# The tail of an attention and routed-MLP kernel: one-tensor statistics, column groups with a pick matmul, ranks by a ones matmul, register-addressed row stores, hinted branches

## The chip, the cores and the metric

One core of a Trainium2 chip. The metric is the time of one execution on the device in microseconds (us), as the median of several executions; beside it stand the range and, where it matters, the mean granted clock of TensorE (1.0 is full speed). Kernels are compared within a call, on one chip, each in turn with the kernel before. A ratio is the mean time of one kernel's fast executions over that of the kernel before in the same rounds, so it is not quite the ratio of the medians that are quoted. "Same" means that the 95% interval of the ratio lies within 2%.

## The reference

Layer norm, attention with 16 query heads on one key and value head, a residual; then a second layer norm and an MLP that runs for only 8 of the 2048 rows, those with the largest router value.

```python
S, D, H, F, C = 2048, 448, 16, 1792, 8          # bf16 throughout
def A(x, wq, wk, wv, wo):                       # attention, one K/V head
    q = heads(x @ wq); k = x @ wk; v = x @ wv
    p = softmax(q @ k.T * (D // H) ** -0.5)
    return merge(p @ v) @ wo
def B(x, w_r, w_gate, w_up, w_down):            # MLP on 8 rows
    r   = x @ w_r
    idx = argsort(-r)[:C]
    y   = (silu(x[idx] @ w_gate) * (x[idx] @ w_up)) @ w_down
    return x.at[idx].add(y * sigmoid(r[idx]))
h  = x + A(layernorm(x), ...)
h2 = h + B(layernorm(h), ...)
```
(Shortened: batch dimension and index arithmetic left out. The second statement uses the layer norm both as input and as residual of B.)

## The kernel before: the parts concerned

The kernel gives every instruction to a small planner (`G.op`: engine, function, estimated duration in ns, what it reads and writes), which orders each engine's program. 281 exponentials on ScalarE carry the attention; VectorE and GpSimd make a share of the exponentials by integer arithmetic. When the last query block is done, the 8 rows are chosen and the MLP runs. TensorE is given matmuls on zeros where the plan shows it idle.

```python
# statistics of one tile of 128 rows, 15 times (in the trace: L752)
G.op(DV, lambda e: e.scalar_tensor_tensor(st[:, t, 6:7], mv[:, t, 0:1], -1.0, st[:, t, 4:5],
                                          ALU.mult, ALU.mult), 80, ...)
# candidates of the first 15 tiles: cast of their router values, transpose, top 8 of each, two small DMAs
G.op(DV, lambda e: e.tensor_copy(rp[:, 0:NT1], r_col[:, 0:NT1]), 80, ...)
...
dma(crow[0:1, :].rearrange("o (t k) -> o t k", k=8), c8[:, :], ["crow"], reads=["c8"])
...
dma(cidx[:, :], i8f[:, :], ["cidx"], reads=["i8f"])
# after the last tile: rank of each candidate, one-hot matrices, selected rows
G.op(DV, stt(scr128[0:8, :], ps[0:8, rbank, 0:128], cols[:, 2:3], onesb[0:8, :], ALU.is_gt, wst[0:8, 9:10]), 280, ...)
# ... gate and up projections on four column groups, silu, product, transposes ...
for h in range(2):                      # down projection: 16 matmuls, 8 columns of the array each
    pieces([mm(ps[0:8, dbank, 0:D], guT[0:CK, k, 32 * c:32 * c + 8], wd_sb[0:CK, 4 * c + k, :],
               k == 0 and c == 0, k == 3 and c == 3) for k in (2 * h, 2 * h + 1) for c in range(4)], 8, 189, ...)
...
G.op(DV, lambda e: e.tensor_copy(base8, ps[0:8, 2, 0:D]), 531, ...)
G.op(DV, lambda e: e.scalar_tensor_tensor(rows8, ps[0:8, dbank, 0:D], fin[:, 1:2], base8, ALU.mult, ALU.add), 540, ...)
evs.append(G.op(PO, lambda e: e.indirect_dma_start(out=out[0], out_offset=...(ap=idx2[:, 0:1], axis=0),
                                                   in_=rows8, ...), 1000, ...))
# at the end of every engine: a flag decides whether an exact second program has to run
bad = e.value_load(flag[0:1, 0:1])
with e.If(bad != 0):
    ...
```
(Cuts are marked with dots.)

## Time and profile before

| | before |
|---|---|
| time, 3 executions | 393.47 us (393.27 to 393.99) |
| span of the profiled execution (it took 394.32 us, more than these three) | 392.5 us, mean granted clock 0.991 |
| first exponential starts, last one ends | 10.06, 370.77 us |
| tail, from there to the end of the span | 21.74 us |

What bounds the kernel is read in the prediction.

```profile
PEclk9999999999999999999999999999999999799999
```

The one slice below 9 is the 35th, where ScalarE has its only two gaps of over 0.3 us after the start.

### The profile page before, as it was taken

Reading aid. Unit: us, or ns where it says so; the run is one execution under the profiler, and the core shown is the slowest. Engines: PE = TensorE matmul, PEld = TensorE weight load, DVE = VectorE, ACT = ScalarE, POOL = GpSimd, SP = SyncE. Lnnn points to the kernel's source line nnn. Section 1 sums busy time; section 2 is a strip of 40 time slices with the busy share of each in tenths; the row PEclk is TensorE's granted clock in tenths of the full one; section 3 lists DMA queues with packets and bytes.
Section 4 is the critical chain, followed back from the end, with each engine's and each line's share of the span. In section 5 each row is a group of like instructions: output and inputs, shape, how many; then the busy total and the mean of one; then the engine's idle time right before and its main releaser. Section 6 shows DMA issues by size and latency. Waiting matters only on the chain.

```text
span 392.5 us, 8604 instructions
## 1 busy us (share of the span) xinstructions
PE 319.9 (82%) x3501; PEld 110.6 (28%) x3501; DVE 338.5 (86%) x695; ACT 366.7 (93%) x307; POOL 193.4 (49%) x180
## 2 busy tenths in 40 slices
PE   8899887878787888878787878888787878788794
PEld 4454322323232222223231322222232312122242
DVE  6995888989898998989898989989898989879872
ACT  5799999999999999999999999999999999799850
POOL 7410135646555464656365454646563654456410
PEclk9999999999999999999999999999999999799999
DMA  7993000010102010100102010100101020100110
GB/s 210 234 244 86 11 17 15 14 52 4 63 5 63 3 52 13 34 33 5 61 3 65 3 63 4 49 16 29 39 4 62 3 65 3 60 3 3 47 42 10
DMA packets 19892, 17.59 MB, mean 45 GB/s; under 512 B 6326, under 2 KB 17094, under 8 KB 19846
## 3 DMA queue, kind: packets, MB, share of 16 engines
q1 hardware_dynamic: 19781, 16.95, 15.8%
q8 instruction: 30, 0.49, 0.6%
q14 instruction: 17, 0.13, 0.1%
q0 software_dynamic: 64, 0.02, 0.0%
HBM read 11.44 MB, written 5.53 MB: 43 GB/s over the span
## 4 chain that ended last, share of the span: by engine, by line
DVE 60%; PE 23%; ACT 12%; issue 4%; POOL 0%; POOLq 0%
DVE Y L910 28%; PE ps L478 22%; ACT P L885 12%; DVE Y L919 11%; DVE st L752 2%; DVE Q L596 2%; DVE hbuf L730 2%; DVE Ot L932 2%; DVE junk L766 2%; DVE bn L734 2%; DVE bn L609 1%; DVE xnT L653 1%; DVE xx L638 1%; DVE mv L735 1%; DVE K L670 1%
## 5 line engine op out<-in xcount | busy, mean ns | idle before, releaser
L885 ACT ACTIVATE P<-ps 128x1536 bf16<-128x1536 f32 (+1 forms) x281 | 355.2, 1422 | 5.0 <-PE ps L478 4.5
L910 DVE TENSOR_SCALAR Y<-ps 128x512 int16<-128x512 f32 x240 | 164.0, 683 | 32.7 <-PE ps L478 32.6
L921 POOL TENSOR_TENSOR Y<-Y,step 128x1024 int32<-128x1024 int32 x60 | 113.5, 1892 | 142.7 <-DVE Y L919 142.1
L478 PE MATMUL ps<-Q,K 32*128 32x512 bf16 x1024 | 111.5, 385 | 62.6 <-DVE Y L910 45.8
L478 PE MATMUL ps<-Y,Vs 128*32 128x512 bf16 x960 | 89.6, 387 | 2.4 <-DVE Y L919 0.5
L478 PEld LDWEIGHTS ps<-Q,K 32*128 32x128 bf16 x1024 | 33.2, 91 | 177.8 <-ACT P L885 160.2
L919 DVE TENSOR_SCALAR Y<-Y 128x2048 int16<-128x2048 int16 x120 | 82.3, 696 | 0.6
L478 PE MATMUL ps<-P,Vs 128*32 128x512 bf16 x784 | 73.0, 388 | 0.0
L478 PE MATMUL ps<-zero 128*32 128x512 bf16 (+3 forms) x162 | 51.4, 395 | 1.2 <-DVE zero L497 1.2
L478 PEld LDWEIGHTS ps<-Y,Vs 128*32 128x32 bf16 x960 | 23.3, 94 | 33.3 <-issue 17.9
L713 POOL TENSOR_TENSOR On<-Ot,Rb 128x256 bf16<-128x256 f32 x28 | 19.8, 727 | 15.2 <-DMA Rb<-l_scr 15.2
L478 PEld LDWEIGHTS ps<-P,Vs 128*32 128x32 bf16 x784 | 18.8, 94 | 28.7 <-issue 26.7
L738 POOL TENSOR_TENSOR st<-st,nhalf 128x1 f32<-128x1 f32 x15 | 17.8, 1185 | 4.6 <-DVE st L736 4.6
L478 PEld LDWEIGHTS ps<-zero 128*32 128x32 bf16 (+1 forms) x162 | 14.4, 101 | 14.8 <-issue 7.5
L478 PE MATMUL ps<-xnT,wq_pad 112*128 112x128 bf16 x256 | 17.4, 220 | 0.0
L758 POOL TENSOR_SCALAR xx<-hbuf,st 128x448 bf16<-128x448 f32 x15 | 15.6, 1041 | 0.0
L478 PEld LDWEIGHTS ps<-xnT,wq_pad 112*128 112x128 bf16 x256 | 14.4, 98 | 3.6 <-issue 3.4
L478 PE MATMUL ps<-wo_pad,On 128*128 128x448 bf16 x64 | 15.0, 355 | 0.0
L755 POOL TENSOR_SCALAR xx<-hbuf,st 128x448 bf16<-128x448 f32 x15 | 11.2, 746 | 1.6
L730 DVE TENSOR_TENSOR hbuf<-ps,xx 128x448 f32<-128x448 f32 x15 | 9.4, 623 | 2.3 <-PE ps L478 2.3
L596 DVE TENSOR_SCALAR Q<-ps,qone 128x512 bf16<-128x512 f32 x15 | 11.2, 744 | 0.0
L752 DVE SCALAR_TENSOR_TENSOR st<-mv,st 128x1 f32<-128x1 f32 x15 | 11.1, 738 | 0.0
(179 smaller groups left out, 170.1 us busy)
## 6 DMA issues: line engine op xcount, KB each, us to landing
Rb<-l_scr SPq DMA_DIRECT2D x14, 256.0 KB
x_scr<-xx SPq DMA_DIRECT2D x15, 224.0 KB, 2.5
out_dram<-xx SPq DMA_DIRECT2D x16, 112.0 KB, 1.7
wg_sb<-in_B_w_gate_dram SPq DMA_DIRECT2D x1, 1568.0 KB, 14.3
wu_sb<-in_B_w_up_dram SPq DMA_DIRECT2D x1, 1568.0 KB, 20.5
wd_sb<-in_B_w_down_dram SPq DMA_DIRECT2D x1, 1568.0 KB, 25.4
xx<-in_A_x_dram SPq DMA_DIRECT2D x3, 448.0 KB, 5.5
wq_sb<-in_A_wq_dram SPq DMA_DIRECT2D x2, 196.0 KB, 2.9
```

The costliest lines, as they stand in the source:

```text
L478: return lambda e: e.matmul(o, lhsT=l, rhs=r, start=start, stop=stop)
L596: G.op(DV, lambda e: e.tensor_scalar(Q[:, q, :, :].rearrange("p g n -> p (g n)"), ps[:, bank, :], qone[:, 0:1], None, ALU.add), dvt(512), ...
L713: G.op(PO, lambda e, c=c: e.tensor_tensor(On[:, rb, c], Ot[:, rb, c], Rb[:, rb, c], ALU.mult), 750, reads=[both[h], rk[h]], writes=[("On", ...
L730: G.op(DV, lambda e: e.tensor_tensor(hbuf[:, hr, :], ps[:, bank, 0:D], x_sb[:, t, :], ALU.add), dvt(D), reads=[pk(bank), ("x", t)], writes ...
L738: G.op(PO, lambda e: e.tensor_tensor(st[:, t, 4:5], st[:, t, 7:8], nhalf[:, 0:1], ALU.pow), 600, reads=[("st7", t), "nhalf"], writes=[("st ...
L752: G.op(DV, lambda e: e.scalar_tensor_tensor(st[:, t, 6:7], mv[:, t, 0:1], -1.0, st[:, t, 4:5], ALU.mult, ALU.mult), 80, reads=[("mv", t), ...
L755: G.op(PO, lambda e: e.tensor_scalar(outf[:, t, :], hbuf[:, hr, :], st[:, t, 5:6], st[:, t, 6:7], ALU.mult, ALU.add), 800, reads=[("h", hr ...
L758: G.op(PO, lambda e: e.tensor_scalar(xn[:, t, :], hbuf[:, hr, :], st[:, t, 4:5], st[:, t, 6:7], ALU.mult, ALU.add), 800, reads=[("h", hr), ...
L885: G.op(AC, lambda e: e.activation(P[:, s0:s0 + w, :], ps[:, b0:b0 + w, :], ACT.Exp, bias=-(ZERO + SHIFT) * OCT, scale=OCT), w * 427 + 50, ...
L910: G.op(DV, lambda e: e.tensor_scalar(Y[:, y, 0, q, :].bitcast(I16), ps[:, vb, :], 0.0, 32639.0 - STEP[3], ALU.max, ALU.min), dvt(512), rea ...
L919: done = [G.op(DV, lambda e, c=c: e.tensor_single_scalar(y[c].bitcast(I16), y[0].bitcast(I16), STEP[c], ALU.add), 600, reads=r, writes=[(" ...
L921: G.op(PO, lambda e: e.tensor_tensor(y[3].bitcast(I32), y[0].bitcast(I32), step3[:, 0:1].broadcast_to([128, 1024]), ALU.add), 2050, reads= ...
```

## The change

Its intent: shorten the chain after the last exponential, and free the statistics of a form that stands behind GpSimd (up to 1.85 us a call in the profile before, 0.15 at its shortest). In words: a one-column statistic is computed by the form with a per-partition scalar instead of two tensors. Two small DMAs become masked products that matmuls sum. The rank of a candidate is counted by a matmul with ones. The down projection runs on four groups of 32 columns of the array, side by side, each leaving a partial sum; a small fp32 matmul with a "pick" matrix adds the four, scales each row by its sigmoid and adds it to its base row. Eight DMAs with the row number in a register store the rows. Each engine announces its last branch some operations ahead (a hint), to shorten the time from the branch to the next instruction (2.7 us on ScalarE in the profile before). The core of the diff:

```diff
-        G.op(DV, lambda e: e.scalar_tensor_tensor(st[:, t, 6:7], mv[:, t, 0:1], -1.0, st[:, t, 4:5],
-                                                  ALU.mult, ALU.mult), 80,
+        G.op(DV, lambda e: e.tensor_scalar(st[:, t, 6:7], mv[:, t, 0:1], st[:, t, 4:5], -1.0, ALU.mult, ALU.mult),
+             80,
...
-        G.op(DV, lambda e: e.tensor_copy(rp[:, 0:NT1], r_col[:, 0:NT1]), 80, ...)      # router values now go into rp directly
-        dma(crow[0:1, :].rearrange("o (t k) -> o t k", k=8), c8[:, :], ["crow"], reads=["c8"])
+        G.op(DV, lambda e: e.tensor_tensor(spread, bmask, c8[:, :].unsqueeze(1).broadcast_to([NT1, NT1, 8]), ALU.mult), ...)
+        G.op(PE, mm(ps[0:1, VB, 0:NC1], onesb[0:NT1, 0:1], wq_sb[0:NT1, 3, 0:NC1], True, True), 60, ...)
...
-    G.op(DV, stt(scr128[0:8, :], ps[0:8, rbank, 0:128], cols[:, 2:3], onesb[0:8, :], ALU.is_gt, wst[0:8, 9:10]), 280, ...)
+    G.op(PE, mm(ps[0:8, kbank, 0:1], above, onesb[:, 0:1], True, True), 64, ...)
...
-        pieces([mm(ps[0:8, dbank, 0:D], guT[0:CK, k, 32 * c:32 * c + 8], wd_sb[0:CK, 4 * c + k, :],
-                   k == 0 and c == 0, k == 3 and c == 3) for k in (2 * h, 2 * h + 1) for c in range(4)], 8, 189, ...)
+        for k in (2 * h, 2 * h + 1):
+            G.op(PE, [mm(ps[32 * c:32 * c + 32, dbank, 0:D], guT[0:CK, k, 32 * c:32 * c + 32], wd_sb[0:CK, 4 * c + k, :],
+                         k == 0, k == 3) for c in range(4)], 189, mode="V", ...)
...
+    G.op(PE, [mm(ps[:, rbank, 0:1], rep4(128, 0), rsig[:, 1:2], True, False),          # sigmoid of each row, on four groups
+              mm(ps[:, rbank, 0:1], rep4(8, 1), cols[:, 1:2], False, True),
+              mm(ps[0:1, rbank, 8:16], rsig[:, 0:1], ohf[:, 0, 0, 0:8], True, False),  # row numbers, on one partition
+              mm(ps[0:1, rbank, 8:16], cols[:, 0:1], ohf[0:8, 1, 0, 0:8], False, True)], 600, mode="F", ...)
+    G.op(DV, lambda e: e.tensor_scalar(pick8, mask8, ps[:, rbank, 0:1], None, ALU.mult), 90, ...)
...
+    for h, c in enumerate(halves):                                                     # fp32, into the bank of the base rows
+        G.op(PE, mm(ps[0:8, obank[h], 0:224], pick8, part[:, c], False, True), 390, mode="F", ...)
+        G.op(DV, lambda e, h=h, c=c: e.tensor_copy(rows8[:, c], ps[0:8, obank[h], 0:224]), 300, ...)
-    evs.append(G.op(PO, lambda e: e.indirect_dma_start(...), 1000, ...))
+    for j in range(8):                                                                 # four on SyncE, four on ScalarE
+        o = G.op(q, lambda e, j=j: e.dma_start(out[0, bass.ds(row[j], 1), :], rows8[j:j + 1, :]), 60, ...)
...
-                with e.If(bad != 0):
+                go = e.br_ne(bad, 0, on_true="exact_" + eng, on_false="end_" + eng)
+                go.branch_hint(hint)                     # announced {PE: 12, ScalarE: 8, VectorE: 8, GpSimd: 1, SyncE: 6} operations ahead
```
(Cuts are marked with dots; comments behind `#` in the diff are added here. Two further one-column statistics, not shown, change from the two-tensor form in the same way.)

## The prediction

> **What bounds the kernel now.** I read the page's head (busy shares and slices), then the costliest groups with their idle times, then the waits and the timeline of the two places where the bound lets go, last the lines of the closing branch.
>
> ```profile
> PE 319.9 (82%) x3501; PEld 110.6 (28%) x3501; DVE 338.5 (86%) x695; ACT 366.7 (93%) x307; POOL 193.4 (49%) x180
> ACT  5799999999999999999999999999999999799850
> L885 ACT ACTIVATE P<-ps 128x1536 bf16<-128x1536 f32 (+1 forms) x281 | 355.2, 1422 | 5.0 <-PE ps L478 4.5
> ```
>
> ScalarE is the bound until the last exponential ends at 370.8 us: 355.2 us of exponentials and only 5.0 us of idleness before them. Work saved on other engines is worth nothing there, except where ScalarE has to wait. The ACT row dips once inside the loop, in the 35th slice. The timeline shows why:
>
> ```profile
> 334.44 0.15 DVE L750 TENSOR_SCALAR st<-st 128x1 f32<-128x1 f32 x1
> 334.44 1.89 POOL L921 TENSOR_TENSOR Y<-Y,step 128x1024 int32<-128x1024 int32 x1
> 334.51 1.85 DVE L752 SCALAR_TENSOR_TENSOR st<-mv,st 128x1 f32<-128x1 f32 x1
> ...
> 337.10 0.40 PE L478 MATMUL ps<-Q,K 32*128 32x512 bf16 x4 [2.17 <-DVE Y L910]
> ...
> 337.54 4.04 ACT L885 ACTIVATE P<-ps 128x1536 bf16<-128x1536 f32 x3 [1.35 <-PE ps L478]
> ```
>
> A one-column VectorE operation lasts 1.85 us because it stands behind a GpSimd operation; PE waits 2.17 us for the bank that VectorE frees late, and ScalarE 1.35 us for PE. The table by stretch adds an after-effect: TensorE's granted clock is 1.00 before, 0.79 in 335 to 340 and 0.61 in 340 to 346, and ScalarE waits again at 342.08 (0.50) and 345.27 (0.23).
>
> After 370.8 nothing overlaps: the end is a chain of short steps, 21.7 us long, to the span's 392.5. Its last part:
>
> ```profile
> 384.32 3.19 PE L478 MATMUL ps<-wd_sb,Y 112*8 112x448 bf16 x16
> ...
> 387.55 0.67 DVE L1148 SCALAR_TENSOR_TENSOR Y<-ps,wq_sb,Y 8x448 bf16<-8x448 f32 x1 [2.92 <-PE ps L478]
> 389.22 0.92 POOL L1150 DMA_INDIRECT out_dram<-Y,wq_sb  x1 [11.52 <-DVE Y L1148]
> ```
>
> Sixteen down-projection matmuls, one each 0.189 us, use 8 of the array's 128 columns; then one pass, then a row store through GpSimd which lands 2.8 us after its issue (DMA part of the page). From the end of L1148 (388.22) to the end of the span it is 4.29 us.
>
> [...] of the two kinds side by side,
>
> ```profile
> L750 DVE TENSOR_SCALAR st<-st x15: 140/144/154, 75.7 to 368.2; 128x1 f32<-128x1 f32 x15
> ...
> L752 DVE SCALAR_TENSOR_TENSOR st<-mv,st x15: 147/751/1846, 75.8 to 368.3; 128x1 f32<-128x1 f32 x15
> ```
>
> the first never exceeds 154 ns, the second (two tensors in) has a median of 751.
> [...] Here
>
> ```profile
> L1216 ACTq COMPARE_BRANCH  x1: 45/45/45, 385.0 to 385.0; - x1
> L1216 PEldq COMPARE_BRANCH  x1: 3702/3702/3702, 385.0 to 385.0; - x1
> L1216 DVEq COMPARE_BRANCH  x1: 76/76/76, 388.1 to 388.1; - x1
> ...
> L1190 ACTq DRAIN  x1: 81/81/81, 387.7 to 387.7; - x1
> ...
> L1190 DVEq DRAIN  x1: 96/96/96, 391.3 to 391.3; - x1
> ```
>
> ScalarE reaches its next instruction 2.7 us after its branch, VectorE 3.2 us, PE stays 3.7 us in it. All of that hides today behind the store.
> [...] The trace shows the fp32 reciprocal broadcast (L478, 128x256 f32) as two instructions 0.216 us apart per 256 columns, 0.43 us in all, four times the 0.107 of a bf16 one at full rate (estimate from the 0.215 us pitch of 512 columns).
> [...] In the trace GpSimd starts its DMA instruction 1.00 us after L1148's end and is busy 0.92 us in it; a four-row store on SyncE is 0.49 us of issue and its reader starts 1.7 us after the start of it in the quiet stretches (68.6 to 70.3).
>
> **The change part by part**, all on the clock of the profile before.
>
> (a) Statistics by a one-tensor form. L752 (and its fellows) take the form whose second operand is a per-partition scalar, as L750 has. The 15 calls lose 8.9 us of busy time (11.1 minus 15 x 0.147), but only the one at 334.5 reached ScalarE. Worth: ScalarE's gaps between 336 and 346, 1.35 + 0.50 + 0.23 plus two of 0.06 = 2.2 us. Because everything later hangs on ScalarE, I count it in full.
>
> (b) Candidates of the first 15 tiles. Two tiny SBUF-to-SBUF DMAs (SyncE busy 0.93 and 0.90; `crow` is read at 372.25, 2.8 us after the issue at 369.44) become masked products and two matmuls. They lie beside the end of attention; the gain is indirect. Now On's second half (L716, ready at 374.34 with its reciprocal) starts at 374.98 because VectorE stands in order before it at the copy of `cols`, waiting 0.64 for PE. With the four fp32 matmuls' estimate raised from 250 to 700 and the candidates ready earlier, the order should be mended: about 0.5 of the 0.64.
>
> (c) Ranks by a ones matmul. Out go the 8x128 comparison (0.34 + its accumulator read) and what slipped in behind it: now one-hot 0 ends at 379.38 and one-hot 1 at 380.10. One-hot 1 then follows 0.2 us behind, at about 379.6: 0.5 us.
>
> (d) The 0.60 us copy of the base rows (L1146) sits before the two copies of guT; it disappears, since base and product now meet in PSUM, and the first guT copy goes to ScalarE (0.36 by its 128x224 neighbour). Down projection starts at about 384.05 instead of 384.32: 0.27.
>
> (e) Down projection on four column groups. The gate projection in the same form: 16 matmuls from 380.957 to 381.898, pitch 0.189 for four. So 0.94 instead of 3.19: -2.25. Added instead of one pass of 0.67: copy of the partial sums in two halves, 0.37 each from the 0.41 of 128x256 (L937), start to start 0.34; the fp32 pick of 224 columns, 2 x 0.189 + 0.16 drain = 0.55; the copy to bf16 0.37 (half of 8x448 at 0.60, plus the fixed part). On the path: 0.03 + 0.34 + 0.38 (second partial) + 0.05 + 0.50 + 0.04 + 0.36 = 1.7. From start of down to rows ready 2.64 instead of 3.90: 1.26.
>
> (f) Store. Out: 4.29 us from rows ready to the end. In: four row stores each on SyncE and ScalarE, addresses already in registers. Issue pitch 0.5 us (SyncE's loads at the start stand 0.5 apart; address arithmetic included by guess): the fourth starts at +1.6, lands 1.67 later (the four-row store), then 0.47 to the end as now (392.04 to 392.51): 3.75. Gain 0.54, not the 1.9 us that leaving GpSimd suggests, because the fixed landing stays and four issues queue up.
>
> (g) Hints. They gain nothing against today's end; they prevent a loss. Without them ScalarE would issue until +2.0, read the flag (0.47) and pay 2.7: +5.2, worse than today's 4.29. With them it is done near +2.6. I take them to work.
>
> Sum: 2.2 + 0.5 + 0.5 + 0.27 + 1.26 + 0.54 = 5.3 us. 393.47 - 5.3 = 388.2; I say **388.4**, since new small operations at the start and in the candidate stage have to cost something.
>
> **The rivals.**
> 1. *Only the tail counts.* The planner makes a new order, and a VectorE/GpSimd collision of another sort (L716 already once lasted 1.35 us; the new masked products have two SBUF inputs) opens a similar gap, so (a) returns nothing. For it: a collision depends on a few tens of ns. Against it: all 15 calls of the one operation that stalls regularly are converted. 390.5.
> 2. *The branch or the stores become the end.* Hints come too late for ScalarE, or the register-addressed stores need 0.9 us each like the two tiny DMAs above. For it: those 0.93 and 0.90 exist; instruction blocks of 8 and 16 KB occupy DMA engines for 0.3 to 1.3 us in the same stretch. Then (f) becomes a loss of 0.6 to 1.5: 389.5 to 390.3.
> 3. *The column groups are hidden anyway.* If the fp32 pick or its weights were held up by the sigmoid and pick arithmetic, (e) would shrink. Against: that arithmetic ends by 381.0 today, 3 us before. At most 0.5 lost: 388.9.
> 4. *More than summed.* If the earlier candidates free all of PE's and VectorE's waits between 372 and 376, another 0.5 to 1: 387.5.
>
> **Range and chances.** (a) is the largest uncertain term, so the lower part of the gain (390.5, with rival 2 mixed in 391) marks the top, full gain plus rival 4 the bottom: 386.8 to 391.0. Faster by over 2% means below 385.6, 7.9 us, more than all terms together: 0.04. Slower by over 2% needs a broken main loop: 0.01. Within 2%: 0.95.
>
> **What would show it.** (a) The former L752 at 0.15 to 0.22 us in every call, no ScalarE gap over 0.3 us after 50 us, last exponential near 368.6, clock 1.00 throughout. (b) On's second half right behind its reciprocal. (c) One-hot 1 within 0.3 us of one-hot 0. (e) Down at about 0.94 us, rows ready 2.6 us after its start. (f) Last landing 3.3 us after rows ready, span's end 0.5 later. (g) No engine but SyncE within 0.5 us of the end. A new ScalarE gap in the loop, stores with a pitch near 0.9 us, or a DRAIN over 1 us after a branch that comes last would make it wrong.

(The 0.16 "drain" of (e) can be read in the profile before: a matmul of 448 columns lasts 0.355 us at a pitch of 0.189.)

## The result, and the profile after

388.62 us (388.29 to 389.10, 4 executions) against 393.37 (392.78 to 393.99, 4 executions): ratio 0.988, 95% interval 0.9861 to 0.9899, "same", 4.75 us less. Predicted were 388.4.

The page of the changed kernel, busy times and slices:

```profile
PE 316.5 (82%) x3511; PEld 109.6 (28%) x3511; DVE 333.3 (86%) x700; ACT 365.4 (94%) x308; POOL 194.7 (50%) x182
...
ACT  4899999999999999999999999999999999999951
...
PEclk9999999999999999999999999999999999999999
...
L914 ACT ACTIVATE P<-ps 128x1536 bf16<-128x1536 f32 (+1 forms) x281 | 354.1, 1510 | 2.6 <-PE ps L493 2.4
```

ScalarE's row has no dip, idleness before the exponentials is 2.6 us instead of 5.0, and the clock row is full. At the place of the gap, the timeline has the same GpSimd operation and the same VectorE term beside it:

```profile
331.97 8.89 ACT L914 ACTIVATE P<-ps 128x1536 bf16<-128x1536 f32 x7
...
333.91 1.89 POOL L950 TENSOR_TENSOR Y<-Y,step 128x1024 int32<-128x1024 int32 x1
...
333.97 0.20 DVE L781 TENSOR_SCALAR st<-mv,st 128x1 f32<-128x1 f32 x1
```

0.20 us where it was 1.85, and seven exponentials without a break. From the 41st to the 263rd exponential, start to start, it is 285.42 us in the profile before and 281.29 after: 4.13 us less, though the gaps that could be read there came to 2.2. Compared start by start, exponential by exponential, the kernel before loses in three parts. By the 257th exponential (334.70 us) it is 1.13 us behind, mostly in eleven steps of 0.07 to 0.09 us, each about 2.05 us after the start of a 0.75 us call of L752, with no gap of ScalarE. At the collision it loses 1.51, over the next five exponentials 1.49.

The tail is 19.33 us instead of 21.74. Its timeline (start, duration, engine, line, operation):

```profile
365.56 1.10 DVE L977 TENSOR_TENSOR wq_sb<-wq_sb,c 15x120 bf16<-15x120 bf16 x1
...
376.47 0.38 PE L493 MATMUL ps<-cols,junk 8*128 8x1 f32 x2
...
377.02 0.94 PE L493 MATMUL ps<-wg_sb,wq_sb 112*32 112x448 bf16 x16
...
380.30 0.94 PE L493 MATMUL ps<-wd_sb,Y 112*32 112x448 bf16 x16
...
381.29 0.69 DVE L1178 COPY Y<-ps 128x224 f32<-128x224 f32 x2 [1.00 <-PE ps L493]
...
381.76 0.92 PE L493 MATMUL ps<-Y,wq_sb 128*8 128x224 f32 x4
...
382.34 0.76 DVE L1212 CAST Y<-ps 8x224 bf16<-8x224 f32 x2 [0.37 <-PE ps L493]
383.26 1.63 ACTq L1217 DMA_DIRECT2D out_dram<-Y  x4
383.30 1.58 SPq L1217 DMA_DIRECT2D out_dram<-Y  x4
```

The down projection takes 0.94 us (3.19 before), the copies, the pick and the last cast follow, and two queues of four row stores each. Step by step, from marker to marker (a marker is the start of the operation named, but for one-hot 1 and the rows ready, which are ends):

| step of the tail | before | after | difference | predicted |
|---|---|---|---|---|
| last exponential's end to the copy of the attention sums | 0.80 | 0.92 | +0.12 | |
| to the statistics of the last tile (On's second half lies here) | 4.61 | 3.86 | -0.75 | -0.5 (b) |
| to its router values | 1.81 | 1.85 | +0.04 | |
| to one-hot 1 | 2.11 | 1.47 | -0.64 | -0.5 (c) |
| to the copy of the selected rows | 0.52 | 0.70 | +0.18 | |
| copy to the start of gate | 0.34 | 0.78 | +0.44 | |
| gate to the start of down | 3.37 | 3.28 | -0.09 | -0.27 (d) |
| down to the rows ready | 3.90 | 2.80 | -1.10 | -1.26 (e) |
| rows ready to the end of the span | 4.29 | 3.67 | -0.62 | -0.54 (f) |
| sum | 21.75 | 19.33 | -2.42 | -3.07 |

The first line of the timeline bears on the first row. This masked product lasts 1.10 us beside GpSimd's 1.89 us operation (from 364.63), its twin behind that operation 0.27. VectorE is then still at this stage when the attention sums are there, which would account for the 0.12. The collision is new, stands in all ten profiles with the masked products (1.10 to 1.16 us), and opens no gap of ScalarE over 0.3 us.

The last lines of each engine, the branch and what comes after it:

```profile
L1283 PEldq COMPARE_BRANCH  x1: 3797/3797/3797, 382.6 to 382.6; - x1
...
L1283 ACTq COMPARE_BRANCH  x1: 68/68/68, 385.6 to 385.6; - x1
...
L1257 ACTq DRAIN  x1: 87/87/87, 386.1 to 386.1; - x1
...
L1257 PEldq DRAIN  x1: 64/64/64, 386.4 to 386.4; - x1
L1257 SPq DRAIN  x1: 13/13/13, 386.5 to 386.5; - x1
```

ScalarE reaches its next instruction 0.5 us after its branch (2.7 before), but PE still sits 3.8 us in it, although its announcement is executed at 379.29, 3.3 us before the branch. Why is not shown (see a_end). PE, SyncE and the last landing (385.95) come within 0.6 us of each other at the end.

### The profile page after: what moved, and what is told of

It reads as the page before. It is cut to its first block, busy times and chain, and to the rows that moved or that the text cites. A ratio compares the mean times of both kernels' runs of the same rounds, so it can differ in the third digit from the quotient of the medians.

```text
span 386.8 us, 8664 instructions
## 1 busy us (share of the span) xinstructions
PE 316.5 (82%) x3511; PEld 109.6 (28%) x3511; DVE 333.3 (86%) x700; ACT 365.4 (94%) x308; POOL 194.7 (50%) x182
## 4 chain that ended last, share of the span: by engine, by line
ACT 84%; DVE 7%; PE 6%; DMA 1%; SPq 1%; issue 1%
ACT P L914 83%; PE ps L493 5%; DVE bn L638 2%; DMA xx<-in_A_x_dram 1%; DVE xnT L682 1%; SPq L519 1%; DVE xx L667 1%; DVE K L699 1%; DVE Y L939 1%; DVE mv L640 0%; PE ps L496 0%; DVE var L661 0%; ACT xx L653 0%; DVE Y L1212 0%; DVE Y L948 0%
## 5 line engine op out<-in xcount | busy, mean ns | idle before, releaser
L948 DVE TENSOR_SCALAR Y<-Y 128x2048 int16<-128x2048 int16 x120 | 81.4, 689 | 0.6
L493 PE MATMUL ps<-zero 128*32 128x512 bf16 (+2 forms) x159 | 48.5, 381 | 1.2 <-DVE zero L512 1.2
L493 PEld LDWEIGHTS ps<-zero 128*32 128x32 bf16 (+1 forms) x159 | 13.6, 98 | 14.1 <-issue 6.6
L787 POOL TENSOR_SCALAR xx<-hbuf,st 128x448 bf16<-128x448 f32 x15 | 16.3, 1086 | 0.0
L638 DVE BATCH_NORM_STATS2 bn<-xx 128x6 f32<-128x448 bf16 x16 | 9.8, 613 | 2.4 <-DMA xx<-in_A_x_dram 2.4
L784 POOL TENSOR_SCALAR xx<-hbuf,st 128x448 bf16<-128x448 f32 x15 | 11.4, 757 | 0.0
```

Source lines behind the costliest of these rows:

```text
L493: return lambda e: e.matmul(o, lhsT=l, rhs=r, start=start, stop=stop)
L638: G.op(DV, lambda e, t=t: e.bn_stats(bn6[:, t, :], x_sb[:, t, :]), dvt(D), reads=[("x", t)], writes=[("bn6", t)])
L784: G.op(PO, lambda e: e.tensor_scalar(outf[:, t, :], hbuf[:, hr, :], st[:, t, 5:6], st[:, t, 6:7], ALU.mult, ALU.add), 800, reads=[("h", hr ...
L787: G.op(PO, lambda e: e.tensor_scalar(xn[:, t, :], hbuf[:, hr, :], st[:, t, 4:5], st[:, t, 6:7], ALU.mult, ALU.add), 800, reads=[("h", hr), ...
L948: done = [G.op(DV, lambda e, c=c: e.tensor_single_scalar(y[c].bitcast(I16), y[0].bitcast(I16), STEP[c], ALU.add), 600, reads=r, writes=[(" ...
```

## The experiments

The theory after reading both profiles: about 4 us come from the loop, because the one-column term no longer stands behind GpSimd, and about 2.4 from the tail. Some 0.6 us of that seemed lost at the start. Rivals: the gain of the loop is the new order's and not the operation's; the tail's parts are hidden behind others; the clock differs for reasons of its own. Twelve kernels ran, all with right results. Where the mean of the executions at full clock is given, it is over those with a mean granted clock of 0.998 or more; this sorting is a coarse one. In 13 of the 14 profiles the clock is also halved at the very end, from 2.3 to 5.3 us after the last matmul on, which costs no matmul anything but lowers the mean: the profile of a_down1 has 0.997 and that of a_nohint 0.994 without any other fall. An execution at 0.996 or 0.997 can thus be an undisturbed one. And the start varies: the x tile that is waited for lands at 6.99 to 8.49 us in these profiles. So a mean of two or three executions is good to about half a microsecond.

### b_ts: the kernel before with the one-tensor form alone

```diff
-        G.op(DV, lambda e: e.scalar_tensor_tensor(st[:, t, 6:7], mv[:, t, 0:1], -1.0, st[:, t, 4:5], ALU.mult, ALU.mult), 80,
+        G.op(DV, lambda e: e.tensor_scalar(st[:, t, 6:7], mv[:, t, 0:1], st[:, t, 4:5], -1.0, ALU.mult, ALU.mult), 80,
```

> The kernel before with one edit: the 15 calls that compute minus mean times rstd take the form with a per-partition scalar instead of two tensors; same duration in the planner, so the same order on every engine. Theory A (the collision of that call with GpSimd at 334.5 us stalls the loop): the calls last 0.15 to 0.22 us each, no ScalarE gap of over 0.3 us between 50 us and the end of attention, clock 1.00 throughout, and the time falls by 2.2 to 4.1 us (2.2 is the sum of the visible gaps, 4.1 what ScalarE's starts gained between the two profiles in the loop): 389.3 to 391.2. Rival B (the main loop's gain comes from the new order of operations): unchanged, 393.0 to 393.8.

Measured: 393.13 us (392.63 to 394.43), ratio 0.9988 (0.9967 to 1.0009). Exponentials 41 to 263: 281.61 us, so the stretch is repaired, and the eleven small steps are gone. But the time did not move. Its timeline shows where the gain went:

```profile
364.54 1.89 POOL L921 TENSOR_TENSOR Y<-Y,step 128x1024 int32<-128x1024 int32 x1 [1.53 <-DVE Y L919]
364.56 1.90 DVE L943 CAST rp<-r_col 128x15 bf16<-128x15 f32 x1
...
366.52 0.27 PE L478 MATMUL ps<-ident,rp 128*15 128x128 bf16 x1 [1.60 <-DVE rp L943]
...
367.38 1.45 ACT L885 ACTIVATE P<-ps 128x1536 bf16<-128x1536 f32 x1 [1.49 <-PE ps L478]
```

Another small operation, a cast of 15 columns, now begins 20 ns after GpSimd's instruction and lasts as long as that; PE's transpose waits 1.60 us in order for it, and ScalarE 1.49. In the profile before the same cast took 0.17 us at 368.32, 0.03 us ahead of GpSimd's at 368.35. What follows: in the order before, part (a) alone is worth next to nothing, because the collision is passed on.

### b_ts2: the same, and the cast removed

```diff
 (as b_ts, and)
-        G.op(DV, lambda e: e.tensor_copy(rp[:, 0:NT1], r_col[:, 0:NT1]), 80, reads=[("r", t) for t in range(NT1)], writes=["rp"])
-            ... e.tensor_scalar(r_col[:, t:t + 1], st[:, t, 3:4], st[:, t, 4:5], -1.0, ...
+            ... e.tensor_scalar(rp[:, t:t + 1], st[:, t, 3:4], st[:, t, 4:5], -1.0, ...
-        ... e.scalar_tensor_tensor(r_col[:, t:t + 1], st[:, t, 6:7], sw[:, 0:1], st[:, t, 2:3], ...
+        ... e.scalar_tensor_tensor(rp[:, t:t + 1], st[:, t, 6:7], sw[:, 0:1], st[:, t, 2:3], ...
```

> The kernel before with the one-tensor form for the term st6 (as the earlier run of that edit) and, besides, the router values written into their bf16 matrix directly, so that the 128x15 cast which lasted 1.90 us in that run no longer exists. Theory (the loop part of the change is worth about 4 us, once both small VectorE operations that can stand behind GpSimd are gone): exponentials 40 to 262 start to start 281.3 to 281.8 us, no ScalarE gap over 0.4 us between 50 us and the last exponential, tail 21.5 to 22.0, time 389.4 to 390.3, ratio to before 0.989 to 0.992. Rival (some other small operation falls into the next collision, the place is what matters and not the operation): a gap of over 1 us again between 330 and 370, time 391.5 to 393.5.

Measured: 390.68 us (390.24 to 391.14), ratio 0.9934 (0.9902 to 0.9966), against 393.01 of the kernel before. Loop 281.48 us and tail 21.72 us lie in the expected ranges, and no ScalarE gap over 0.4 us is left between 50 us and the last exponential. The time, 2.3 us less, is not: 389.4 to 390.3 had been expected, from the 4 us of two profiles. So the change needs both removals for its loop part, and that part is worth less in the median than in the profile.

### a_stt: the changed kernel with the two-tensor form put back

```diff
-        G.op(DV, lambda e: e.tensor_scalar(st[:, t, 6:7], mv[:, t, 0:1], st[:, t, 4:5], -1.0, ALU.mult, ALU.mult), 80,
+        G.op(DV, lambda e: e.scalar_tensor_tensor(st[:, t, 6:7], mv[:, t, 0:1], -1.0, st[:, t, 4:5], ALU.mult, ALU.mult), 80,
```

> The changed kernel with the same 15 calls put back to the two-tensor form, order as in the changed kernel. Theory A: calls of 0.7 us and more come back, and if one of them again stands behind the 1.9 us GpSimd pass when PE has nothing else, 2 to 4 us come back: 390.6 to 392.6. Rival B: within 0.4 us of the changed kernel, 388.2 to 389.0. Between the two: calls stall 0.75 us again, but the one long stall needs the old order, 388.6 to 389.5.

Measured: 392.71 us (392.06 to 395.06), ratio 0.997 (0.995 to 0.999). The loop is back at 285.24 us, the term lasts 1846 ns at 335.6 and ScalarE has a gap of 1.24 us at 337.4:

```profile
L781 DVE SCALAR_TENSOR_TENSOR st<-mv,st x15: 150/752/1846, 76.3 to 368.4; 128x1 f32<-128x1 f32 x15
```

In the new order, too, the operation makes the gap. The eleven steps of 0.09 us are back as well, each about 2.05 us after the start of a 0.75 us call; no profile without the two-tensor form has them. None of the six executions had the full clock.

### a_nohint: without the announcements of the branches

```diff
-                go.branch_hint(hint)
```

> The changed kernel without the branch hints, all else the same. My step (g): ScalarE's first instruction after the branch comes 2.6 to 2.8 us after it instead of 0.42, so that ScalarE ends last and the time rises by 1.9 to 2.3 us, to about 390.7; VectorE's comes 3 us after its branch and hides; PE's branch stays at 3.8 us with or without the hint. Rival: [...] nothing changes, 388.6.

Measured: 391.06 us (390.46 to 392.16), ratio 0.9929 (0.991 to 0.9948), so about 2.4 us by the medians more than the changed kernel of the first comparison, and 3.2 in the profile. SyncE and ScalarE after the branch:

```profile
L1257 SPq DRAIN  x1: 13/13/13, 386.9 to 386.9; - x1
L1257 ACTq DRAIN  x1: 66/66/66, 389.7 to 389.7; - x1
```

ScalarE branches at 386.0 and is at its next instruction at 389.7: 3.7 us, where it is 0.5 with the announcement. The prediction had taken 2.7 for it; the three profiles of the old kernel and its variants have 2.5 to 2.9. ScalarE ends the kernel here, as (g) said it would.

### a_down1: the sixteen down matmuls on one column group

```diff
-            G.op(PE, [mm(ps[32 * c:32 * c + 32, dbank, 0:D], ..., k == 0, k == 3) for c in range(4)], 189, mode="V", ...
+            G.op(PE, [mm(ps[0:32, dbank, 0:D], ..., k == 0 and c == 0, k == 3 and c == 3) for c in range(4)], 756, mode="F", ...
-        G.op(DV, lambda e, c=c: e.tensor_copy(part[:, c], ps[:, dbank, c]), ...
+        G.op(DV, lambda e, c=c: e.tensor_copy(part[0:32, c], ps[0:32, dbank, c]), ...
```
(The pick then sums over one group of 32.)

> The changed kernel with the 16 down-projection matmuls on one column group one after the other (rows 0 to 31 of the bank, partial copies and pick over 32 partitions), all else the same. Theory: the 16 take 3.2 us instead of 0.94, the end moves by 2.2 to 2.3 us, 390.9. Rival (what follows hides it, for example ScalarE and SyncE or PE's branch): less than 1.5 us.

Measured: 391.61 us (390.22 to 392.94), ratio 0.9945 (0.9918 to 0.9972); in the profile the tail is 21.63 us, 2.3 more than with four groups. Nothing else takes the place of the longer matmuls: the 2.25 us that the groups save lie on the path. At full clock it is 390.31 (2 executions), 1.9 above the changed kernel; with the profiled one, which had no fall before its last matmul, 390.53 and 2.15.

### a_start: the bias of tile 1 ahead of the statistics of tiles 2 and 3

```diff
+    for t in (2, 3):
+        bnop[t].deps[bnop["v"].idx] = False        # order on VectorE, no semaphore
```

> The changed kernel with the statistics of x tiles 2 and 3 ordered behind the bias of tile 1 on VectorE, so that K of tile 0 and that bias no longer stand behind the late landing of tiles 2 and 3. Theory (the changed kernel lost 0.6 to 0.7 us at its start to this order and this landing, and the start counts in full because ScalarE is the bound from its first exponential): first exponential at 9.9 to 10.3 us instead of 10.79, time 0.4 to 0.7 less than the changed kernel, 387.9 to 388.3. Rival (a later wait at the start, for the same late tiles, takes it back within the first 20 us): first exponential earlier, but exponential number 40 no earlier, time 388.5 to 388.8.

The first exponential starts at 10.79 us in the changed kernel and at 10.06 in the one before. Measured here: 9.72, and the lead stays (41st exponential at 59.57 instead of 60.48). The executions at full clock are 387.69 and 387.84, the median is 388.53 (387.55 to 390.76), ratio 0.9899 (0.9858 to 0.994). So the order gains 0.6 us by these two executions. By the profile it is 0.3: tile 2 landed at 7.49 here, from which the old order starts 2.57 later, at 10.06. But my reason for the late start was wrong. In a_prep2, whose start has the changed kernel's order, tile 2 landed at 6.99 us instead of 8.21 and the first exponential started at 10.08; in b_ts2, with the order before, they are at 8.16 and 10.73. In ten of the profiles with the old start order, of both kernels, the exponential comes 2.57 or 2.58 us after that landing wherever it is the landing that is waited for. The landing varies by more than 1 us from execution to execution; the change did not cause it.

### a_prep2: the matmuls of the scaled pick matrix behind the up projection

```diff
-    G.op(PE, [ (four fp32 matmuls) ], 600, mode="F", ...)
+    G.op(PE, [ (the two for the row numbers) ], 250, mode="F", ...)
+    G.op(PE, [ (the two for the sigmoids) ], 450, mode="F", deps=up[-1:], ...)
```

> The changed kernel with the two fp32 matmuls that make the scaled pick matrix put behind the up projection on PE (the two for the row numbers stay where they are). Theory (these fp32 matmuls stand in front of the gate projection and took away most of what the shorter ranks gave): copy of the transposed selected rows to gate start 0.4 to 0.5 us instead of 0.78, tail 18.9 to 19.1 instead of 19.33, time 388.2 to 388.4. Rival (moved to the other side they delay the transposes or the pick): down projection starts no earlier or rows ready comes 0.2 to 0.4 later after it, time 388.5 to 389.

Measured: 388.45 us (387.69 to 391.08), ratio 0.99 (0.9859 to 0.9942). From the copy to gate it is 0.35 us instead of 0.78, as expected; the tail is 19.19 us, only 0.14 less. The rest went here:

```profile
375.97 0.94 PE L493 MATMUL ps<-wg_sb,wq_sb 112*32 112x448 bf16 x16
...
378.24 0.32 PE L496 MATMUL ps<-ident,Y 128*112 128x128 bf16 x2
...
378.86 0.32 PE L496 MATMUL ps<-ident,Y 128*112 128x128 bf16 x2
```

The two pairs of transposes are 0.62 us apart; in the changed kernel they are 0.27 apart. With the moved matmuls, half of the base rows' matmuls fell between them. So the fp32 matmuls do hold up gate, and moved behind it they make another hold-up: the theory about the place is confirmed, the gain isn't. The three executions at full clock, 387.69 to 387.95, have a mean 0.56 below the changed kernel's; in the profiled one the shorter tail and an early start (10.08 us instead of 10.79) cover that.

### a_pool: the old store by GpSimd

```diff
-    for j in range(8): ... e.dma_start(out[0, bass.ds(row[j], 1), :], rows8[j:j + 1, :]) ...
+    G.op(PO, lambda e: e.indirect_dma_start(out=out[0], out_offset=...(ap=idx1[:, 0:1], axis=0), in_=rows8, ...), 1000, ...)
```

> The changed kernel with the old store: one indirect DMA by GpSimd, the row numbers on 8 partitions; everything else kept, hints too. Theory (the register-addressed stores are worth the difference of the two profiles, 4.29 against 3.67 us from rows ready to the end): 4.2 to 4.4 us from rows ready to the end, time 389.0 to 389.4. Rival (with all engines done early and hinted the old store would end as soon, the gain is the hints' alone): 388.5 to 388.8.

Measured: 389.65 us (388.26 to 391.94), ratio 0.9903 (0.9868 to 0.9939). In the profile it is 4.08 us from rows ready to the end, a little under the expected 4.2 to 4.4. The two executions at full clock, 388.92 and 389.15, are 0.65 above the changed kernel's, but one at 0.997 took 388.26, no more than that kernel itself. The profiles decide: the register-addressed stores are worth 0.4 us, 4.08 against 3.67, a little less than (f) had.

This profile (391.94 us) had a tail of 22.61 us although its program is as short: down takes 1.68 us instead of 0.94, because the granted clock is 0.5 from 377.75 to 384.58. That asks what makes the clock fall.

### What makes the clock fall

The falls ahead of the last matmul last 3.413 or 6.827 us in all profiles, one length or twice that. So I cut the profiles into windows of 3.413 us, on the grid that the edges of the falls give. The kernel before, by stretches on that grid (busy us of each engine, then the granted clock):

```profile
core 0: us, PE busy (x) PEld busy (x) DVE busy (x) ACT busy (x) POOL busy (x), PEclk, DMA share, GB/s
...
334.47:337.88 3.41, 1.24 (x20) 0.25 (x12) 2.98 (x5) 2.06 (x3) 3.28 (x3) 1.00 0.00 0
337.88:341.29 3.41, 3.09 (x24) 0.52 (x20) 2.47 (x7) 3.30 (x3) 0.00 (x0) 0.50 0.39 114
341.29:344.71 3.42, 3.42 (x23) 0.63 (x19) 2.67 (x4) 2.86 (x3) 1.25 (x1) 0.50 0.19 66
```

PE waits 2.17 us for the late bank in the first stretch and runs at half clock for the two that follow. How idle a window is before a fall the page doesn't say. I worked out a share for each window, an estimate: a matmul counts its moving columns at the rate of the trace (0.215 us for 512, to within 1%), twice that for each instruction of an fp32 one (0.216 us for 256 columns), the double at half clock (0.39 to 0.42 us for 512 in the fall above), and overlaps count once. The first stretch above comes to 0.28. In the ten profiles at hand, every window at full clock with 0.412 or less was followed by a fall and none with 0.423 or more. What ends a fall is open: of the six in all profiles three lasted two windows. "Busy" in the page is no substitute: in a window of after_again (below) it is 2.86 of 3.41 us where the share is 0.39, and a matmul of 8 moving columns counts there with 0.17 us (changed kernel, 376.78 to 376.93).

With the same sum the grid can be shifted over a profile, since it lies differently in each execution. In the kernel before, windows that begin between 332.8 and 335.8 us have 0.412 or less, 3.0 of the 3.41 us. In the changed kernel nothing is left in the loop, but three places in the tail have it, at 365.7 to 366.0, 366.8 to 367.2 and 373.3 to 374.2; on the grid they cover 1.3 of 3.41 us. In b_ts2 there is none, and its six executions lie within 0.9 us of each other (the two at 0.996 are not the slow ones). This was put to the test:

### after_again: the changed kernel as a control

No edit.

> The changed kernel once more, unaltered, as the control of the three others on the same chip. Theory (the granted clock falls to 0.5 for 3.41 or 6.83 us after a 3.41 us window in which matmuls stream for 0.41 or less of the time, as in all earlier profiles; windows with 0.42 or more do not set it off; the grid of windows lies differently in each execution, and the changed kernel's tail has places, window starts at 365.4 to 366.0, 366.7 to 367.2 and 373.2 to 374.3 us, where such a window can fall): its six times fall in two groups, 388.2 to 389.0 at a mean clock of 0.998 or more and 390 to 391.5 at 0.990 to 0.995, two to four of six in the second. Rival (the falls of the clock are not tied to the kernel's own activity): no two groups, or falls in all four kernels of this call alike.

Measured: 388.27 us (388.05 to 390.02), ratio 0.9874 (0.9854 to 0.9895). Only one of the six, not two to four, is in a second group: 390.02 at clock 0.995. It happens to be the profiled one (columns as in the table above):

```profile
366.94:370.35 3.41, 2.86 (x21) 1.73 (x17) 2.09 (x12) 1.47 (x4) 1.19 (x2) 1.00 0.32 101
370.35:373.77 3.42, 3.09 (x16) 1.58 (x17) 1.30 (x6) 0.80 (x3) 1.20 (x1) 0.50 0.04 7
373.77:377.18 3.41, 3.19 (x18) 1.27 (x16) 3.20 (x19) 2.33 (x5) 0.31 (x1) 1.00 0.02 4
```

A window that begins at 366.94, in the second of the three places, with a share of 0.39, and half clock for the next one. The tail is 1.4 us longer than in the other profile of the same program. The place and the share were as expected; how often was not.

### a_fill: more matmuls on zeros in the last block and the tail

```diff
-            if self.recent(s) >= self.FLOOR0:
-                return None                                   # in the tail: fill wherever the plan has room
-        if ... self.recent(s) >= (self.FLOOR if b else self.FLOOR0):
+        if ... self.recent(s) >= (self.FLOOR0 if b in (0, max(self.todo)) else self.FLOOR):
```

> The changed kernel with more idle-time matmuls on zeros in the last attention block and in the tail (one more of 512 columns and some small ones; nothing else). Theory (low windows set off the half clock): no execution with a mean clock under 0.996, all six times within 388.2 to 389.2, so a median up to 2 us below the control's if the control falls into the second group. Rival (not tied to activity, or the added matmuls stand in the way): a second group near 390.5 to 391.5 here too, or all times 0.3 us or more above the control's first group.

Measured: 387.83 us (387.39 to 388.81), ratio 0.9868 (0.9846 to 0.989). All six have 0.998 or more and there is no second group. Against one of six in the control that alone shows little. One such place of 0.65 us remains by the same sum. Four of the times lie below the expected range; in the profiled one tile 2 landed at 7.03 us, an early start.

### a_end: the flag read ahead of the stores, PE's branch announced 60 operations ahead

```diff
-HINT = {PE: 12, AC: 8, DV: 8, PO: 1, SP: 6}
+HINT = {PE: 60, AC: 8, DV: 8, PO: 1, SP: 6}
+            if o.name == "store" and self.bad is None:        # SyncE and ScalarE
+                e.wait_ge(self.flag_sem, self.flag_val)
+                self.bad = e.value_load(self.flag_t[0:1, 0:1])
```

> The changed kernel with SyncE and ScalarE reading the flag before their stores instead of behind them, and PE's branch hint 60 operations ahead instead of 12. Theory (the end of the changed kernel is a near tie of SyncE's own sequence, of PE's branch and of the landings, 386.4, 386.5 and 386.0 on its clock): PE's branch lasts under 0.6 us instead of 3.8, SyncE's flag read of 0.6 us leaves the path, rows ready to the end 3.2 to 3.4 us instead of 3.67, and executions at full clock 388.0 to 388.3 instead of 388.6. Rival (the hint does nothing for PE[...]): PE's branch still near 3.7 us and the end with it, 388.5.

Measured: 388.75 us (387.75 to 390.26), ratio 0.9887 (0.9859 to 0.9914); at full clock 387.99 (3 executions).

```profile
L1291 PEldq COMPARE_BRANCH  x1: 474/474/474, 382.6 to 382.6; - x1
```

PE's branch takes 0.47 us instead of 3.8, and 0.39 in a_best. Rows ready to the end is 3.46 us instead of 3.67, not the 3.2 to 3.4 hoped for: the last landing, at 386.04, is now what the end follows. These are two edits at once, but other profiles separate them. With PE's announcement 12 operations ahead, its branch lasted 3.4 to 3.9 us in five profiles, 1.23 in a_prep2, 0.47 in a_pool and 1.09 in after_again:

```profile
L1283 PEldq COMPARE_BRANCH  x1: 1094/1094/1094, 383.9 to 383.9; - x1
```

There, as in the first profile of this program, the announcement came 3.3 us before the branch; so its distance alone does not decide. And rows ready to the end was 3.69 us in a_prep2 and 3.77 in after_again: a short branch of PE shortens nothing. So the 0.2 us come from the flag read. Three of six executions were at 0.991 to 0.995 and 389.1 to 390.3.

### a_best: all four together

The edits of a_start, a_prep2, a_end and a_fill.

> All four together: bias of tile 1 ahead of the statistics of tiles 2 and 3, pick matmuls behind the up projection, flag and PE hint early, and the filling matmuls. Sum of the parts at full clock: 388.6 minus 0.4 (start) minus 0.3 (pick) minus 0.4 (end) = 387.5, and no second group from the clock: all six within 386.9 to 388.0. Rival (the parts stand in each other's way, the filling matmuls delay the tail by up to 0.5): 388.0 to 388.5.

Measured: 387.54 us (387.21 to 388.58), ratio 0.9859 (0.9837 to 0.9881). Five of six are within the expected 386.9 to 388.0, the sixth, 388.58, is at clock 0.995. It is 0.73 us below the control by the medians; the intervals of the ratios overlap, so it is probably but not surely the faster one.

### What the sorting by clock gives

At full clock: before 392.64 us (12 executions of 32 fast ones, 392.13 to 393.22), b_ts2 390.80 (4), after 388.38 (6, of the first comparison and the control). The other 20 of before have a mean of 393.88. The kernels with the changed kernel's tail unfilled (the changed kernel, a_start, a_end) have 8 of 22 executions at 0.995 or less, near the 38% that 1.3 of 3.41 us would give; the two filled ones have 1 of 12, which fits the theory but is too few to show it. For the kernel before, 3.0 of 3.41 would be 88%, and 20 of 32 are below 0.998, 63%: no profile of it at full clock was taken, so whether the collision is shorter there is open. One execution of before, at 460.58 us and clock 0.56, was slow in another way and is left out, as in the ratios.

## Why the prediction was right, point by point

The time was right within 0.2 us, and the mechanisms held. The terms:

- **(a), 2.2 us, had its size from the wrong parts.** The collision is real, and the two-tensor form causes it (a_stt). But "only the one at 334.5 reached ScalarE" is wrong: the shorter calls cost eleven steps, about 1.0 us together, without a gap that a list of waits would show. The gaps of 0.50 and 0.23 that the prediction added came while the clock was halved (337.88 to 344.71), when the exponentials were 1.51 us apart instead of 1.33; that these 1.49 us belong to the clock is a reading of the traces, which no run separates, but in a_stt, with a fall of one window instead of two, it was 0.73. At full clock the loop part is worth 1.8 us (392.64 minus 390.80). If the small steps are in it, the collision itself is worth about 0.8 there (an estimate from these numbers), less than its 1.51 in the profile. The prediction saw the clock in the table and called it an after-effect; its step "I count it in full" took one execution for all. That 2.2 lies near 1.8 is luck: a loss not seen and a loss that only some executions have nearly cancel.
- **(a) also needed part of (b).** The prediction credited the operation alone. b_ts shows that without the removal of the cast the gain is lost to the next collision; rival 1 described this, for another operation, and the change happened to have it covered. Its own example came true too, the masked product of 1.10 us, but at a place where it cost 0.12 at most.
- **(b) and (c), 1.0 us: 1.39 at their own steps**, but 0.62 were given back at once, between one-hot 1 and gate. 0.44 of them are the fp32 matmuls for pick matrix and row numbers, which stand on PE ahead of gate. No rival named this. Rival 3 is the nearest: it had feared that such arithmetic would hold up the pick.
- **(d), 0.27: 0.09.** The copy of the base rows did disappear. From the end of the first pair of transposes to the start of down it is 0.57 us instead of 0.79. But that end comes 2.71 us after the start of gate instead of 2.58, with matmuls for the base rows and the flag just ahead of the transposes on PE. No run takes this apart.
- **(e), 1.26: 1.10**, and a_down1 confirms that it lies on the path.
- **(f), 0.54: 0.62** between the two profiles, of which a_pool gives the stores 0.4. Two of its terms were off and cancel. The fourth store starts 1.56 us after the rows are ready (1.6 predicted; the mean pitch is 0.45 us on SyncE and 0.47 on ScalarE). It lands 1.29 later, not 1.67, but from there to the end it is 0.82 instead of 0.47: SyncE, behind its stores, still reads the flag (0.58 us) and branches. That is the path which a_end shortens. Rival 2 did not come true.
- **(g)** holds for ScalarE: without announcements 2.4 us by the medians. PE's announcement did not take effect in this profile, so that PE ends 0.3 us before the span, against the sign that no engine but SyncE would be within 0.5. It costs nothing: where PE's branch was short (after_again, a_prep2) the end came no sooner.
- **The sum.** 5.3 were added up; 4.3 is what the executions at full clock show (392.64 to 388.38), 4.75 what the medians of the first comparison show, 5.7 what the two profiles show. The prediction of 5.1 came close because the time that it started from had the falls of the clock in it, and the term (a), read from a profile with such a fall, contained part of them. That is partly luck. Rival 4, more than the sum, did not come true.

## What to carry to other kernels

Before summing gaps from one profile, look whether the granted clock fell in it, and mark which gaps come after the fall; compare executions of the same clock. Compare two profiles start by start: small delays need not leave a gap. A small VectorE operation with two tensors in, or a cast, that starts just behind a long GpSimd one is a risk (1.85 and 1.90 us here, behind GpSimd's 1.89): remove all of its kind in that stretch, or the next takes over, as in b_ts. In a tail, try whether filling TensorE's idle time keeps the clock up (not shown here: 1 of 12 executions at 0.995 or less with the filling, 8 of 22 without), announce a branch ahead (ScalarE's next instruction came 0.5 us after it instead of 3.7), and see in the profile whether the announcement took effect.

## What was measured of the hardware

- The granted clock: the window before the fall in the kernel before holds a wait of 2.17 us and a share of 0.28; windows in which matmuls streamed for 0.39 to 0.41 of the time were followed by the half clock too, while none of 0.42 or more was (in all 14 profiles, from 22 us to the last matmul, among windows at full clock 6 with a fall, the largest share 0.412, and 1,455 without, the smallest 0.423). The share is an estimate, worked out as above.
- The closing branch: 2.5 to 3.7 us from branch to next instruction on ScalarE and 2.8 to 3.2 on VectorE without an announcement (four profiles), 0.5 and 0.6 with it (ten profiles, but for ScalarE in a_pool: 3.6 in spite of it). PE's branch takes 3.3 to 3.7 without, 0.5 to 3.9 with one 12 operations ahead, 0.4 to 0.5 with one 60 ahead (two profiles).
- Small VectorE operations beside GpSimd: the cast of 128x15 took 1.90 us behind GpSimd's 1.89, 0.17 elsewhere; the `tensor_scalar` of one column took 0.20 us in all 15 calls, one of them beside GpSimd's 1.89.
- Row stores whose address is in a register: four on one queue took 1.58 us (SyncE) and 1.63 us (ScalarE), and the last landed 1.3 us after its issue.
